# Fixed places for the splits and stores of weight forms, four rounded tiles in layer one, and token-form remainders on VectorE

## The chip, the cores and the metric

The kernel runs on one core of one Trainium2 chip. The metric is the device time of one execution in microseconds. The engines are called TensorE (PE), VectorE (DVE), ScalarE (ACT), GpSimd (POOL) and SyncE (SP); ScalarE and SyncE also issue the transfers of this kernel.

## What is computed

Attention in a window of 128 tokens with a linear bias (4 batches, 8 heads, 576 tokens, 64 per head), then a gated layer (512 to 1536 and back to 512) and a second layer whose two products are multiplied and go through two more weights:

```python
attn = softmax(where(mask, q @ k.T / 8 + bias, -1e9))     # 4 x 8 heads
x = (attn @ v).transpose(0, 2, 1, 3).reshape(2304, 512)
x = (sigmoid(x @ w_gate) * (x @ w_val)) @ w_out           # layer one, 1536 wide
out = ((x @ w1) * (x @ w2) @ w3) @ w_out2                 # layer two, 1024 wide
```

## The kernel before

**Precision.** A float32 operand is split into two parts that TensorE takes at full rate: `act_copy` (L79) writes the rounded high part on ScalarE, `dve_lo` (L82) or `pool_lo` (L85) subtracts it and writes the remainder on VectorE or GpSimd. Each product then has three passes (L31): high by high, high by low, low by high. Weights come as 64-bit words; `rounded` (L140) makes float32 of them with one ScalarE step (L146, absolute value) and six VectorE steps (L147 to L152) into a tile with the tag `ca`, of which there are two. Some weights are rounded ahead and stored to `early32` in DRAM; they come back as float32 (`raw32`).

**Stages.** Attention runs to about 180 us with parts of layer one beside it. Layer one (`gv`, `down1`) runs over slices 0 to 11 of its width, in groups of two, and five blocks of tokens of 256 or 512; the products `gv` go through a tanh (`g`, L364), a multiply (L371) and a split (`gt`), and `dn` adds into `acc` (L398). Near its end the fold (`fold`, L299) multiplies the two last weights into `outd`, and `x_forms(0)` makes sums and differences of the token blocks, split into `xf` (L422 to L426). With n = 0 its remainders go to GpSimd for B11, B21, T1 and T3, and to VectorE for the others.

**Layer two** runs over slices 12 to 19, twice (n = 0 with token blocks 1, 2 and 0, n = 1 with blocks 3 and 4). For each slice `products` (L454) forms seven products by a scheme that needs sums and differences of the weights: eight weight forms A21, A22, A11, A12, S1 to S4, kept as high and low parts in a tile `forms`. There are two such tiles, one for even and one for odd slices. The chunks of a slice follow one another on TensorE: `pb` with A11, `pd` with S1, `pb` with S2, `pb` with S3, `pc` with A12, `pb` with A22, `pd` with S4. Three of them add into the same bank, and ScalarE copies the bank in between: `x1` after A11, `xa` after S2, `xb` after S3. A chunk into `pb` can't start before the copy of what stood there. The products of x1 and of xa with xb are split into `tp` and `tq` (`turn`, L468) and feed the output products `o` (`down2`, L539), which stand between the chunks of the following slices. `lone` (L513) does block 0.

**How the forms come.** With n = 0 `form_sink` (L207) is called by `convert_next` (L155), right behind the rounding, for the slice two ahead of the one whose products were just issued. It splits A11 with A12 and A21 with A22, adds and subtracts on VectorE (L225 to L228) and splits S1 with S2 and S3 with S4: four ScalarE copies and four GpSimd subtracts. `keep` (L232) stores the forms to DRAM from ScalarE's queue, and `again` (L247) loads them for n = 1.

**What sets the order.** A planner puts the instructions of each engine in order by priority and by its own estimate of when they can start; each engine then works its queue in that order. `tc.high_priority(offset=SOONER)` moves instructions ahead, `LATER` (in `convert_next`) moves them back. `tc.issue_after(ins)` ties the instructions of a block that run on the engine of `ins` behind `ins` in that queue. Outside attention the order of TensorE too is the planner's.

Of the kernel before, what the change touches and what calls it, by code (L numbers as in the profile page):

```python
# [56 lines left out]
def attn_moe_kernel(  # L57
# [19 lines left out]
    NK = DM // P  # L77

    def act_copy(dst, src):  # L79
        nc.scalar.activation(dst, src, AF.Copy)  # L80

    def dve_lo(dst, src, hi):  # L82
        nc.vector.tensor_tensor(dst, src, hi.bitcast(F32), ALU.subtract)  # L83
# [1 line left out]
    def pool_lo(dst, src, hi):  # L85
        nc.gpsimd.tensor_tensor(dst, src, hi.bitcast(F32), ALU.subtract)  # L86
# [22 lines left out]
        return accpools[blk > 1].tile(shape, F32, tag=f"acc{blk}", name=f"{name}_{blk}")  # L109


    spool = None
    staged = {}
    rings = {"raw": 2, "raw32": 0, "ca": 2}
    held = {"raw": 0, "raw32": 0}
# [13 lines left out]
    def kind(src):  # L129
        return "raw32" if src.dtype == F32 else "raw"  # L130
# [9 lines left out]
    def rounded(t, key):  # L140

        low, high = t[:, :, 0], t[:, :, 1]
        a = spool.tile([P, DM], U32, name=f"a_{key}", tag="ca", bufs=rings["ca"])
        s = spool.tile([P, DM], U32, name=f"s_{key}", tag="cs", bufs=1)
        x, y = a.bitcast(F32), s.bitcast(F32)
        nc.scalar.activation(x, high.bitcast(F32), AF.Abs)  # L146
        nc.vector.tensor_scalar(x, x, bits(F64_LEAST), bits(F64_MOST), ALU.max, ALU.min)  # L147
        nc.vector.tensor_scalar(a, a, 0x07FFFFFF, 3, ALU.bitwise_and, ALU.logical_shift_left)
        nc.vector.scalar_tensor_tensor(a, high, 0xC0000000, a, ALU.bitwise_and, ALU.bitwise_or)
        nc.vector.tensor_scalar(s, a, 0xFF800000, None, ALU.bitwise_and)  # L150
        nc.vector.scalar_tensor_tensor(y, low, 2.0**-52, y, ALU.mult, ALU.mult)
        nc.vector.tensor_tensor(x, x, y, ALU.add)  # L152
        return x

    def convert_next():  # L155

        key, src, sink = queue.pop(0)
        with tc.high_priority(offset=-LATER):
            t = staged.pop(key)
            held[kind(src)] -= 1  # L160
            x = t if t.dtype == F32 else rounded(t, key)
            if sink is None:
                nc.sync.dma_start(ahead[key[1:]], x)
            elif (to := sink(key, x)) is not None:
                hi, lo = to
                act_copy(hi, x)
                (dve_lo if key[0] in ("o2", "w3") else pool_lo)(lo, x, hi)
        fetch_more()
# [17 lines left out]
    def parts(grp):  # L186
        def src(i, c):
            m = i - NF
            own = (w_gate, w_val, w_out)[c][i] if i < NF else (w1[m], w2[m])[c]
            return ahead.get((i, c), own)  # L190

        if grp[0] >= NF:
            return [((i, c), src(i, c), form_sink) for i in grp for c in range(2)]
        keys = [(i, c) for c in range(3) for i in grp]
        return [(key, src(*key), part_sink) for key in keys]

    forms = {}
    half = {}
    form_tiles = {}
    outw = {}  # L200

    def form_tile(i):
# [4 lines left out]
    def form_sink(key, x):  # L207

        i, c = key
        x = x.rearrange("p (b c) -> p b c", b=2)  # L210
        if c == 0:
            forms[i] = form_tile(i)
            half[i] = x
        w = forms[i]

        def split(at, src):
            hi, lo = w[:, at : at + 2, 0], w[:, at : at + 2, 1]
            act_copy(hi, src)
            pool_lo(lo, src, hi)

        split(A11 if c == 0 else A21, x)
        if c == 1:
            a = half.pop(i)
            s12, s34 = (upool.tile([P, 2, 2 * P], F32, name=f"s{k}_{i}", tag="cf", bufs=2) for k in (12, 34))
            nc.vector.tensor_tensor(s12[:, 0], x[:, 0], x[:, 1], ALU.add)  # L225
            nc.vector.tensor_tensor(s12[:, 1], s12[:, 0], a[:, 0], ALU.subtract)
            nc.vector.tensor_tensor(s34[:, 0], a[:, 0], x[:, 0], ALU.subtract)
            nc.vector.tensor_tensor(s34[:, 1], a[:, 1], s12[:, 1], ALU.subtract)  # L228
            split(S1, s12)
            split(S3, s34)  # L230
# [185 lines left out]
    def x_forms(n):  # L416

        p, q = (acc[blk] for blk in PAIRED[n])
        some_lo = dve_lo if n else pool_lo
        b11, b21, b12, b22 = p[:, 0:2], p[:, 2:4], q[:, 0:2], q[:, 2:4]  # L420

        def split(j, src, lo):  # L422
            t = xf[n, j] = xpool.tile([P, 2, 2, TB], F32R, name=f"xf{n}_{j}", tag=PLACES[n][j])
            for h in range(2):
                act_copy(t[:, 0, h], src[:, h])
                lo(t[:, 1, h], src[:, h], t[:, 0, h])  # L426

        def minus(to, x, y):
            for h in range(2):
                nc.vector.tensor_tensor(to[:, h], x[:, h], y[:, h], ALU.subtract)  # L430

        split(B11, b11, some_lo)
        yield
        split(B21, b21, some_lo)
        yield
        split(B22, b22, dve_lo)
        yield
        minus(b12, b12, b11)
        split(T1, b12, some_lo)
        yield  # L440
        minus(b22, b22, b12)
        split(T2, b22, dve_lo)
        yield
        minus(b11, b22, b11)
        split(T3, b11, some_lo)
        yield
        minus(b21, b21, b22)
        split(T4, b21, dve_lo)
        yield
# [4 lines left out]
    def products(n, i):  # L454

        def chunk(ps, a, j, first, last):
            for kk in range(2):
                for wp, xp in PASSES:
                    nc.tensor.matmul(  # L459
                        ps, forms[i][:, a, wp, kk * P : (kk + 1) * P], xf[n, j][:, xp, kk],  # L460
                        start=first and kk == 0 and (wp, xp) == PASSES[0],
                        stop=last and kk == 1 and (wp, xp) == PASSES[-1], skip_group_check=True,
                    )

        def bank(name, pool, tag):
            return pool.tile([P, TB], F32, tag=tag, name=f"{name}{n}_{i}", bufs=4)

        def turn(pr, name):  # L468
            t = m2.tile([P, 2, TB], F32R, tag="gt", name=f"{name}{n}_{i}", bufs=4)
            act_copy(t[:, 0], pr)  # L470
            pool_lo(t[:, 1], pr, t[:, 0])
            return t

        def now():
            return tc.high_priority(offset=SOONER)

        ts = ts2[n, i] = {}
        b, d = bank("pb", gvpool, gvtag), bank("pd", gvpool, gvtag)
        x1 = m2.tile([P, TB], F32, tag="g", name=f"x1_{n}_{i}")
        x2a, x2b = (upool.tile([P, TB], F32, tag="u", name=f"{nm}{n}_{i}") for nm in ("xa", "xb"))  # L480
        chunk(b, A11, B11, True, False)
        with now():
            act_copy(x1, b)
        yield 0
        chunk(d, S1, T1, True, False)
        yield 1
        chunk(b, S2, T2, False, False)
        with now():
            act_copy(x2a, b)
        yield 2  # L490
        chunk(b, S3, T3, False, False)
        with now():
            act_copy(x2b, b)
            nc.vector.tensor_tensor(x2b, x2b, d, ALU.add)
        yield 0
        c = bank("pc", mmpools[0], "mm")
        chunk(c, A12, B21, True, True)
        with now():
            nc.vector.tensor_tensor(x1, x1, c, ALU.add)
        yield 3  # L500
        chunk(b, A22, T4, False, True)
        with now():
            nc.vector.tensor_tensor(x1, x1, b, ALU.mult)
            ts[PAIRED[n][0]] = turn(x1, "tp")
        yield 1
        chunk(d, S4, B22, False, True)
        with now():
            nc.vector.tensor_tensor(x2a, x2a, d, ALU.add)
            nc.vector.tensor_tensor(x2a, x2a, x2b, ALU.mult)
            ts[PAIRED[n][1]] = turn(x2a, "tq")  # L510
        yield 1

    def lone(i):  # L513

# [321 lines left out]
        attention(actx, conv)  # L836


    rings.update({"raw": 3, "raw32": 4, "ca": 2})
    spool = ctx.enter_context(tc.tile_pool(name="conv1", bufs=1, reuse_waits="tile"))  # L840
    w3st = ExitStack()
    w3pool = w3st.enter_context(tc.tile_pool(name="w3pool", bufs=3, side="right", reuse_waits="tile"))
    w1st = ExitStack()
    wpools.append(w1st.enter_context(tc.tile_pool(name="wpool1", bufs=2, reuse_waits="tile")))
    gvpool = ctx.enter_context(tc.tile_pool(name="psgv", bufs=4, space=PSUM, reuse_waits="tile"))
    gvtag, gvbufs = "gv", 4
# [45 lines left out]
    flush()  # L892
    formpools = [None, None]
    w1st.close()
    upool = ctx.enter_context(tc.tile_pool(name="upool", bufs=3, reuse_waits="tile"))
    formpools[0] = ctx.enter_context(tc.tile_pool(name="forms0", bufs=1, reuse_waits="tile"))
    second = groups[last1 + 1 :]
# [16 lines left out]
    for n in range(len(PAIRED)):  # L914
        for g, grp in enumerate(second):
            final = n == 0 and g + 1 == len(second)
            for at, i in enumerate(grp):
# [3 lines left out]
                for gap in products(n, i):  # L921
# [3 lines left out]
                        step(alone)  # L925
                    if i == slices[-1] and n == 0:
                        step(xform)
                if n == 0:
                    with tc.issue_after(folded[NM - 1].ins):
                        keep(i)  # L930
                if at:
                    for _ in downs:
                        pass
# [64 lines left out]
```

## Time and profile before

| | us |
|---|---|
| median of 3 runs (lowest to highest) | 922.53 (921.52 to 926.82) |
| profiled execution | 922.87 |
| its span, first to last instruction | 921.2 |
| TensorE busy in the span | 877.7 |
| VectorE, ScalarE, GpSimd busy | 665.9, 352.4, 322.8 |

In the rows further down, a timeline has one line for each instruction (or for several alike): start in us, length in us, engine, line, operation, output `<-` inputs, shapes, count, and in brackets the idle time before it and what ended it. A mean clock of 1.00 is 2.4 GHz; 0.5 would be 1.2 GHz.

### The profile page before, as it was taken

The numbers are of one execution on the slowest core, as the hardware profiler recorded it, in microseconds if no ns is written. First come the engines' busy times: TensorE is split into PE (matmuls) and PEld (weight loads), VectorE is DVE, ScalarE is ACT, GpSimd is POOL, SyncE is SP. The second block draws the span as 40 slices with busy tenths as digits, with TensorE's granted clock in tenths as the row PEclk, the third lists the DMA queues.
The fourth block names the chain that finished last, engine by engine and source line by source line (L and its number), as shares of the span: only waits on it lengthen the run. The fifth ranks groups of instructions, "written<-read, shape, count | busy, mean of one in ns | idle before, by whom it ended". The sixth has DMA issues, their size and how long they took to land. (4 is left out here: it accounts for less than half of the span.)

```text
span 921.2 us, 12491 instructions
## 1 busy us (share of the span) xinstructions
PE 877.7 (95%) x4432; PEld 718.6 (78%) x4432; DVE 665.9 (72%) x1148; ACT 352.4 (38%) x853; POOL 322.8 (35%) x360
## 2 busy tenths in 40 slices
PE   6788998999999999999999899999989999999998
PEld 4556776788888888888888788878877788888886
DVE  6879898579994985986898872794587748534444
ACT  6878666533322322322332343443433324122120
POOL 4766554543312312412321223224744332112121
PEclk7899898999999999999999999999999999999999
DMA  5445352243440341251245441238454143655322
GB/s 200 144 144 183 116 187 80 77 141 106 139 159 1 115 153 42 86 164 60 69 129 168 148 138 38 78 128 316 185 206 148 82 168 95 227 192 175 105 102 92
DMA packets 40623, 121.67 MB, mean 132 GB/s; under 512 B 4464, under 2 KB 6512, under 8 KB 38512
## 3 DMA queue, kind: packets, MB, share of 16 engines
q1 hardware_dynamic: 39264, 106.05, 35.0%
q10 hardware_dynamic: 1296, 14.81, 3.8%
q8 instruction: 35, 0.57, 0.3%
q14 instruction: 28, 0.23, 0.1%
HBM read 88.34 MB, written 32.51 MB: 131 GB/s over the span
## 5 line engine op out<-in xcount | busy, mean ns | idle before, releaser
L347 PE MATMUL gv<-xth,wsl 128*128 128x512 f32 (+1 forms) x960 | 283.1, 373 | 3.3 <-DVE g L371 2.5
L347 PEld LDWEIGHTS gv<-xth,wsl 128*128 128x128 f32 x960 | 177.4, 192 | 37.4 <-issue 3.0
L347 PE MATMUL gv<-xtl,wsl 128*128 128x512 f32 (+1 forms) x480 | 178.4, 372 | 0.4 <-DVE xtl L83 0.4
L388 PE MATMUL dn<-gt,wsl 128*128 128x512 f32 (+1 forms) x720 | 157.4, 372 | 10.8 <-DVE xtl L83 4.5
L86 POOL TENSOR_TENSOR gt<-g,gt 128x512 fp32r<-128x512 f32 (+1 forms) x60 | 76.3, 1274 | 244.2 <-ACT gt L80 244.1
L388 PEld LDWEIGHTS dn<-gt,wsl 128*128 128x128 f32 x720 | 126.4, 190 | 36.7 <-issue 5.7
L459 PE MATMUL pb<-xf,forms 128*128 128x512 f32 x384 | 99.6, 396 | 6.7 <-ACT xa L80 5.3
L347 PEld LDWEIGHTS gv<-xtl,wsl 128*128 128x128 f32 x480 | 92.2, 192 | 15.9 <-DVE xtl L83 1.2
L459 PEld LDWEIGHTS pb<-xf,forms 128*128 128x128 f32 x384 | 71.2, 190 | 23.1 <-ACT xa L80 7.2
L398 DVE TENSOR_TENSOR acc<-acc,dn 128x512 f32<-128x512 f32 (+1 forms) x120 | 73.4, 626 | 19.5 <-PE dn L388 19.5
L80 ACT ACTIVATE gt<-g 128x512 fp32r<-128x512 f32 (+1 forms) x60 | 35.2, 588 | 96.2 <-DVE g L371 96.2
L559 DVE TENSOR_TENSOR acc<-acc,o 128x512 f32<-128x512 f32 x54 | 36.7, 684 | 39.7 <-PE o L549 39.4
L712 ACT ACTIVATE sm<-sm,mn 128x128 f32<-128x128 f32 x144 | 55.8, 390 | 19.0 <-DVE mn L709 12.9
L371 DVE SCALAR_TENSOR_TENSOR g<-g,gv 128x512 f32<-128x512 f32 (+1 forms) x60 | 37.5, 628 | 35.1 <-PE gv L347 32.4
L86 POOL TENSOR_TENSOR tp<-x,tp 128x512 fp32r<-128x512 f32 x16 | 21.8, 1361 | 94.9 <-ACT tp L80 94.9
L459 PE MATMUL pd<-xf,forms 128*128 128x512 f32 x192 | 48.7, 389 | 0.0
L549 PE MATMUL o<-outw,tp 128*128 128x512 f32 x192 | 47.7, 390 | 0.3 <-POOL tp L86 0.3
L549 PE MATMUL o<-outw,tq 128*128 128x512 f32 x192 | 47.9, 389 | 0.0
L364 ACT ACTIVATE g<-gv 128x512 f32<-128x512 f32 (+1 forms) x60 | 31.9, 546 | 40.9 <-PE gv L347 36.6
L720 POOL TENSOR_SCALAR sm<-sm,su 128x128 f32<-128x128 f32 x72 | 31.8, 453 | 42.7 <-DVE su L716 37.3
L308 PE MATMUL w3o<-wo,w3s 128*128 128x512 f32 x192 | 44.0, 389 | 0.0
L549 PEld LDWEIGHTS o<-outw,tp 128*128 128x128 f32 x192 | 36.0, 188 | 8.2 <-POOL tp L86 0.7
(798 smaller groups left out, 1468.9 us busy)
## 6 DMA issues: line engine op xcount, KB each, us to landing
formd<-forms ACTq DMA_DIRECT2D x8, 1792.0 KB, 6.4
outw<-outd SPq DMA_DIRECT2D x16, 512.0 KB, 6.0
forms<-formd SPq DMA_DIRECT2D x8, 1024.0 KB, 5.2
ldk<-in_k_dram SPq DMA_DIRECT2D x16, 320.0 KB, 3.7
ldv<-in_v_dram SPq DMA_DIRECT2D x16, 320.0 KB, 3.0
out_dram<-acc SPq DMA_DIRECT2D x18, 256.0 KB, 2.0
ldq<-in_q_dram SPq DMA_DIRECT2D x16, 256.0 KB, 4.0
outd<-w3o SPq DMA_DIRECT2D x8, 512.0 KB, 3.4
```

The costliest lines, as they stand in the source:

```text
L80: nc.scalar.activation(dst, src, AF.Copy)
L86: nc.gpsimd.tensor_tensor(dst, src, hi.bitcast(F32), ALU.subtract)
L308: nc.tensor.matmul(acc2, w3s[u][:, wp, i * P : (i + 1) * P], wo2[kk][:, xp], start=(kk == 0 and wp == 0 and xp == 0), stop=(kk == NC2 - 1 ...
L347: nc.tensor.matmul(ps, wsl[i][:, s, wp, kk * P : (kk + 1) * P], xs[blk][xp][:, kk], start=(kk == 0 and wp == 0 and xp == 0), stop=(kk == N ...
L364: nc.scalar.activation(g[i], pss[i, 0], AF.Tanh, scale=0.5)
L371: nc.vector.scalar_tensor_tensor(pr, pr, 1.0, pss[i, 1], ALU.add, ALU.mult)
L388: nc.tensor.matmul(ps, wsl[i][:, 2, wp, m * P : (m + 1) * P], t[:, xp], start=n == 0, stop=n == 3 * len(grp) - 1,)
L398: nc.vector.tensor_tensor(a, a, ps, ALU.add)
L459: nc.tensor.matmul(ps, forms[i][:, a, wp, kk * P : (kk + 1) * P], xf[n, j][:, xp, kk], start=first and kk == 0 and (wp, xp) == PASSES[0], ...
L549: nc.tensor.matmul(ps, ts2[n, i][blk][:, xp, tt * P : (tt + 1) * P], outw[i][:, wp], start=k == 0, stop=k == 3 * len(grp) - 1,)
L559: nc.vector.tensor_tensor(a, a, ps, ALU.add)
L712: s["act"] = nc.scalar.activation(y, y, AF.Exp, bias=mn[:, j : j + 1], scale=1.0 / up, accum_out=su[:, j : j + 1])
```

## The change

For slices 14 to 19, `form_sink` now only keeps the two tiles, and the splits are issued by `make_forms` during the products of the slice before: behind the copy `xb` of slices 14 to 18, and for slice 14 behind the copy `x1` of slice 13. `keep` of slices 14 to 19 is tied behind the copy `xa` of the same slice (that of 12 and 13 behind the last fold, as before). A raw tile that a waiting split still reads counts as held until then. The split of the second product into `tq` is issued behind the next slice's copy `x1`, in both passes, but for the last slice. In layer one there are four tiles `ca` in a pool of their own, and two in layer two. The remainders of all `xf` of `x_forms(0)` are on VectorE.

```diff
     def rounded(t, key):
-        a = spool.tile([P, DM], U32, name=f"a_{key}", tag="ca", bufs=rings["ca"])
+        a = (capool or spool).tile([P, DM], U32, name=f"a_{key}", tag="ca", bufs=rings["ca"])
     def convert_next():
-            held[kind(src)] -= 1
+            if not (kind(src) == "raw32" and sink is form_sink and key[0] > NF + 1):
+                held[kind(src)] -= 1
     def form_sink(key, x):
+        if i > NF + 1:
+            if c == 1:
+                waiting[i] = lambda: (form_part(i, 0, half[i]), form_part(i, 1, x))
+        else:
+            form_part(i, c, x)
+
+    def form_part(i, c, x):
         w = forms[i]
...
     def x_forms(n):
-        some_lo = dve_lo if n else pool_lo
+        some_lo = dve_lo
...
         chunk(b, A11, B11, True, False)
         with now():
-            act_copy(x1, b)
+            copied = act_copy(x1, b)
+        if n == 0 and i == NF + 1:
+            make_forms(i + 1, copied)
+        while late:
+            with now(), tc.issue_after(copied.ins):
+                late.pop(0)()
...
         chunk(b, S2, T2, False, False)
         with now():
-            act_copy(x2a, b)
+            copied = act_copy(x2a, b)
+        if n == 0:
+            with tc.issue_after((copied if i > NF + 1 else folded[NM - 1]).ins):
+                keep(i)
         yield 2
         chunk(b, S3, T3, False, False)
         with now():
-            act_copy(x2b, b)
+            copied = act_copy(x2b, b)
             nc.vector.tensor_tensor(x2b, x2b, d, ALU.add)
+        if n == 0 and NF + 1 < i < NF + NM - 1:
+            make_forms(i + 1, copied)
...
             nc.vector.tensor_tensor(x2a, x2a, x2b, ALU.mult)
-            ts[PAIRED[n][1]] = turn(x2a, "tq")
+            ts[PAIRED[n][1]] = t = m2.tile([P, 2, TB], F32R, tag="gt", name=f"tq{n}_{i}", bufs=4)
+
+        def turn_later():
+            act_copy(t[:, 0], x2a)
+            pool_lo(t[:, 1], x2a, t[:, 0])
+
+        if i == NF + NM - 1:
+            with now():
+                turn_later()
+        else:
+            late.append(turn_later)
...
+    def make_forms(i, after):
+        with tc.issue_after(after.ins):
+            waiting.pop(i)()
+        for c in range(2):
+            if parts_of[i, c] == "raw32":
+                held["raw32"] -= 1
+        fetch_more()
...
-    rings.update({"raw": 3, "raw32": 4, "ca": 2})
+    rings.update({"raw": 3, "raw32": 4, "ca": 4})
     spool = ctx.enter_context(tc.tile_pool(name="conv1", bufs=1, reuse_waits="tile"))
+    w1st = ExitStack()
+    capool = w1st.enter_context(tc.tile_pool(name="capool1", bufs=1, reuse_waits="tile"))
...
     w1st.close()
+    rings["ca"] = 2
+    capool = ctx.enter_context(tc.tile_pool(name="capool2", bufs=1, reuse_waits="tile"))
...
-                if n == 0:
-                    with tc.issue_after(folded[NM - 1].ins):
-                        keep(i)
```

## Rows read from the trace of the kernel before

**Rows 1.** The page's head: span, then busy us, share and instructions of each engine.

```profile
span 921.2 us, 12491 instructions
...
PE 877.7 (95%) x4432; PEld 718.6 (78%) x4432; DVE 665.9 (72%) x1148; ACT 352.4 (38%) x853; POOL 322.8 (35%) x360
```

**Rows 2.** Table of stretches: from:to us, length, busy us of engines, granted clock, transfers.

```profile
250.00:510.00 260.00, 260.00 (x1250) 219.65 (x1249) 210.72 (x345) 74.72 (x127) 70.07 (x53) 1.00 0.34 107
...
520.00:530.00 10.00, 7.47 (x49) 7.18 (x48) 8.56 (x16) 3.46 (x7) 3.01 (x2) 0.84 0.43 145
...
690.00:700.00 10.00, 9.65 (x41) 8.06 (x42) 5.26 (x10) 3.49 (x7) 4.10 (x4) 0.83 0.00 0
```

**Rows 3.** Waits of TensorE, 250 us to the end: us in total, times, longest.

```profile
PE pb L459 <- ACT xa L80: 5.3, 3, 2.4
PE gv L347 <- DVE g L371: 2.5, 1, 2.5
PE pb L459 <- ACT xb L80: 1.4, 1, 1.4
PE dn L388 <- DVE acc L398: 1.4, 1, 1.4
```

**Rows 4.** Timeline of all engines in slices 15 and 16, 680 to 712 us.

```profile
683.20 1.78 DVE L152 TENSOR_TENSOR a_(17, 0)_6430<-a_(17, 0)_6430,s_(17, 0)_6431 128x512 f32<-128x512 f32 x1
...
688.68 0.41 DVE L226 TENSOR_TENSOR s<-s,a_(17, 0)_6430 128x256 f32<-128x256 f32 x1
...
689.18 0.63 ACT L80 ACTIVATE forms<-s 128x512 fp32r<-128x512 f32 x1 [5.94 <-issue]
689.71 0.58 ACT L80 ACTIVATE xa<-pb 128x512 f32<-128x512 f32 x1
...
690.35 2.67 PE L459 MATMUL pb<-xf,forms 128*128 128x512 f32 x6 [2.37 <-ACT xa L80]
...
695.95 0.68 ACT L146 ACTIVATE a_(18, 0)_6603<-raw_(18, 0)_6293 128x512 f32<-128x512 f32 x1 [1.41 <-POOL forms L86]
```

**Rows 5.** Timeline of TensorE, 700 us to the end: A11 of slices 16, 17.

```profile
702.40 1.52 PE L459 MATMUL pb<-xf,forms 128*128 128x512 f32 x6
...
723.30 1.52 PE L459 MATMUL pb<-xf,forms 128*128 128x512 f32 x6
```

**Rows 6.** Timeline of ScalarE, 555 to 665 us: slices 12 and 13.

```profile
644.46 0.63 ACT L80 ACTIVATE forms<-raw_(14, 0)_5875 128x512 fp32r<-128x512 f32 x1 [1.45 <-DMA formd<-forms]
...
645.51 0.58 ACT L80 ACTIVATE xb<-pb 128x512 f32<-128x512 f32 x1
```

**Rows 7.** Timeline of all engines in layer one, 505 to 545 us.

```profile
522.51 0.67 ACT L146 ACTIVATE a_('w3', 7)_5548<-raw_('w3', 7)_5242 128x512 f32<-128x512 f32 x1 [3.56 <-DMA early<-_('ahead', 'w3', 5)_5079]
...
525.21 0.68 DVE L371 SCALAR_TENSOR_TENSOR g<-g,gv 128x512 f32<-128x512 f32 x1
```

**Rows 8.** Timeline of VectorE, 555 to 665 us: end of layer one.

```profile
590.07 1.25 DVE L430 TENSOR_TENSOR acc<-acc,acc 128x512 f32<-128x512 f32 x1
...
605.68 0.68 DVE L83 TENSOR_TENSOR w3s<-raw_('w3', 10)_5521,w3s 128x512 fp32r<-128x512 f32 x1
606.28 0.68 DVE L398 TENSOR_TENSOR acc<-acc,dn 128x512 f32<-128x512 f32 x1
```

**Rows 9.** Timelines of VectorE, ScalarE and GpSimd in slice 16, 706 to 747 us.

```profile
709.20 0.69 DVE L152 TENSOR_TENSOR a_(18, 1)_6616<-a_(18, 1)_6616,s_(18, 1)_6617 128x512 f32<-128x512 f32 x1
...
714.56 0.60 ACT L80 ACTIVATE xb<-pb 128x512 f32<-128x512 f32 x1 [1.47 <-PE pb L459]
...
715.75 1.29 POOL L86 TENSOR_TENSOR forms<-a_(18, 0)_6603,forms 128x512 fp32r<-128x512 f32 x1 [2.02 <-ACT forms L80]
```

**Rows 10.** Groups of VectorE, 588 to 612 us: count, busy us, mean ns.

```profile
L430 DVE TENSOR_TENSOR acc<-acc,acc 128x512 f32<-128x512 f32 x6 | 6.8, 1144 | 0.1
...
L83 DVE TENSOR_TENSOR xf<-acc,xf 128x512 fp32r<-128x512 f32 x6 | 4.9, 831 | 0.0
L430 DVE TENSOR_TENSOR acc<-acc 128x512 f32<-128x512 f32 x2 | 1.4, 688 | 0.0
```

More of the change, by code (lines that the diff above doesn't have):

```diff
@@ L79, in act_copy @@
     def act_copy(dst, src):
-        nc.scalar.activation(dst, src, AF.Copy)
+        return nc.scalar.activation(dst, src, AF.Copy)
     def dve_lo(dst, src, hi):
@@ L109, in acc_tile @@
         return accpools[blk > 1].tile(shape, F32, tag=f"acc{blk}", name=f"{name}_{blk}")
-    spool = None
+    spool = capool = None
     staged = {}
@@ L192, in parts @@
         if grp[0] >= NF:
+            parts_of.update({(i, c): kind(src(i, c)) for i in grp for c in range(2)})
             return [((i, c), src(i, c), form_sink) for i in grp for c in range(2)]
@@ L197, in attn_moe_kernel @@
     forms = {}
+    parts_of = {}
     half = {}
     form_tiles = {}
+    waiting = {}
+    late = []
     outw = {}
@@ L836, in attn_moe_kernel @@
         attention(actx, conv)
-    rings.update({"raw": 3, "raw32": 4, "ca": 2})
+    rings.update({"raw": 3, "raw32": 4, "ca": 4})
     spool = ctx.enter_context(tc.tile_pool(name="conv1", bufs=1, reuse_waits="tile"))
+    w1st = ExitStack()
+    capool = w1st.enter_context(tc.tile_pool(name="capool1", bufs=1, reuse_waits="tile"))
     w3st = ExitStack()
     w3pool = w3st.enter_context(tc.tile_pool(name="w3pool", bufs=3, side="right", reuse_waits="tile"))
-    w1st = ExitStack()
     wpools.append(w1st.enter_context(tc.tile_pool(name="wpool1", bufs=2, reuse_waits="tile")))
```

## The prediction

> **What bounds the kernel now.** I read the page's head first: TensorE is busy 877.7 of 921.2 us [rows 1]. Next came the table of stretches, because an average share hides where the idle time lies. From 250 to 510 us TensorE is busy all the time at a granted clock of 1.00 [rows 2]. So a change to the other engines can gain only in between, and only by ending a wait of TensorE. The list of TensorE's waits from 250 us to the end has four entries over half a microsecond: 5.3 us (three waits) on the copy `xa`, 2.5 on `g`, 1.4 on `xb` and 1.4 on `acc` [rows 3], 10.6 us in sum. The first 180 us, the attention, come before anything that the diff touches.
>
> Idle time is not the whole price. In 520 to 530 us the granted clock is 0.84, in 690 to 700 us it is 0.83 [rows 2]; TensorE had just idled 2.5 and 2.4 us. Part of each stretch thus ran at 1.2 GHz instead of 2.4. That loses 10 x 0.16 = 1.6 and 10 x 0.17 = 1.7 us. The matmuls agree: the six `pb` after the second wait take 2.67 us [rows 4], six of the same kind without a wait 1.52 [rows 5], so 1.15 of the 1.7 us are seen there. What the change can reach is 10.6 + 1.6 + 1.7 = 13.9 us.
>
> Who is late, wait by wait? In slice 15 (679 to 702 us) ScalarE idles 5.94 us and then runs, first, a split `forms<-s` at 689.18 and, behind it, the copy `xa<-pb` at 689.71 [rows 4]. The split belongs to slice 17. It waited for VectorE, whose `s` (L226) ran from 688.68 to 689.09 because rounding stood ahead of it, one step of which (L152) took 1.78 us beside a GpSimd subtract [rows 4]. The copy itself was only queued behind that split, and TensorE's next six `pb` (S3) need the copy. Slices 16 and 17 repeat this, with 5.3 - 2.4 = 2.9 us between them. At 644.46 a split of slice 14 waits 1.45 us for the store of slice 12's forms, and the copy `xb` runs only at 645.51 [rows 6]: the 1.4 us. At 522.51 the rounding's first step waits 3.56 us on ScalarE for a store to `early`, which still holds one of two rounded tiles; VectorE's rounding and behind it the multiply `g` (525.21) follow, and TensorE waits 2.5 us for it [rows 3, 7]. At 606.28 the addition to `acc` that frees a PSUM bank stands behind splits on VectorE [rows 8], which held the last `dn` by 1.4 us.
>
> **The change, part by part.** *Splits behind fixed copies (slices 14 to 19).* No split of slices 14 to 19 is issued two slices ahead any more. Those of slice i+1 follow slice i's copy `xb` (for slice 14, slice 13's copy `x1`). No instruction is added or removed. In slices 15, 16 and 17 nothing that waits for VectorE's rounding is then in front of `xa`. Gain: 5.3 + 1.7 = 7.0 us. The cost must be sought in slice i+1: a slice lasts 723.30 - 702.40 = 20.9 us [rows 5]; the copy `xb` ends about 12.8 us into it (714.56 + 0.60 - 702.40) [rows 5, 9]. Then come four ScalarE copies of 0.63 us [rows 4] and four GpSimd subtracts of some 1.3 us [rows 9], with the subtracts of `tp` and `t` between them: 4 x 1.3 + 1.3 + 0.7 (half the width, so an estimate of half the time) = 7.2 us. That ends 20 us into the slice, in time for slice i+1, which needs only A11 first, S1 1.4 us later and the rest 6 us or more later. So I cost it at nothing; the cover is the tail of slice i.
>
> The rounding must then be done when the splits come. For slice 18 it ran from 695.95 to 709.20 + 0.69, or 13.9 us [rows 4, 9]. Its two tiles come free some 3 us after one `xb` and are wanted at the next, so there are 20.9 - 3 = 17.9 us. Slack: 4 us.
>
> *Stores.* `keep(i)` of slices 14 to 19 now stands behind `xa` of the same slice on ScalarE's queue. By then its forms have long been written, so it waits for nothing; it goes past `xb`, by the length of one issue. The store reads tiles that are overwritten a slice and a half later. SP's queue keeps its order. Cost: nothing; cover: the products between S3 and A22. Slices 12 and 13 keep their old tie to the fold. The store of slice 12 therefore lands as late as before (644.4 us), and the splits of slice 14 still need it. Only what stands behind them may differ. The gain on that 1.4 us lies between 0 and 1.4. I take 0, since the row that ends that wait is not touched.
>
> *The copy `tq` behind the next slice's `x1`.* `x1` of the next slice stood behind `tq`, which waits for VectorE's product. Now it comes first, so S2 can follow S1 sooner. `tq` is wanted only by the later half of the output products. Gain on the path: none shown beyond the 7.0; cost: 0.
>
> *Four rounded tiles in layer one.* The wait of 3.56 us for a slot goes, as two more are free. VectorE's four rounding steps in front of `g` start that much earlier, more than TensorE's 2.53 us of idling. Gain: 2.5 + 1.6 = 4.1 us. From below: 0, if another instruction becomes late in its place, and even a loss of as much, since more rounding may now be in VectorE's queue ahead of a `g`.
>
> *Remainders on VectorE.* Eight subtracts `xf` go from GpSimd (1.3 us each by its other subtracts) to VectorE (0.68) [rows 8, 9]. Four of them stood at 563 to 569 us, where VectorE is nearly idle. The other four fall in 588 to 612 us, where VectorE has no pause. Adding: VectorE's splits there start 0.60 us apart (605.68, 606.28) [rows 8], so 4 x 0.60 = 2.4 us. Removing: beside GpSimd's subtracts the six L430 take 1144 ns on average against 688 undisturbed, the six `xf` 831 against 680 [rows 8, 10]: 6 x 0.456 + 6 x 0.151 = 3.6 us. Some 0.5 of it is the L430 at 590.07 (1.25 us instead of 0.69) [rows 8], which lies beside a `gt` subtract that stays. Net 3.1 - 2.4 = 0.7 us earlier. The wait of 1.4 us falls to 0.7. Bounds: all of it goes (+1.4), or no relief comes and it grows by 2.4.
>
> The Trainium skill (page "SBUF — State Buffer", section "Who interferes with whom") says that a VectorE instruction with two SBUF inputs and a GpSimd instruction that reads SBUF block one another whole, whichever starts first. The 1.78 us beside a GpSimd subtract agree with it [rows 4]. By the rule alone the slices' splits, now in one run on GpSimd, would delay VectorE's rounding more than before, which is the rival below on late rounding.
>
> **The sum.** 7.0 + 0 + 4.1 + 0.7 = 11.8 us. The profiled execution took 922.87 us, its span 921.2; 922.87 - 11.8 = 911.1. The median of the three runs is 0.34 lower, so 910.7.
>
> **The rivals.** (1) *Layer one keeps a wait.* The order of every queue is made anew by the planner, and VectorE is busy 210.7 of 260 us there [rows 2]. Another `g` may come late. Against it: fewer things wait for stores. Time: 910.7 + 4.1 = 914.8. (2) *The change does only part of its work in layer two*: each of slices 14 to 18 keeps a short wait of another kind, say at A22 for `xb`, of 1.4 us, like the two waits of slices 16 and 17 (2.9 / 2). Five of them cost 7.0: 917.7. (3) *Nothing is gained*: both happen, 921.8. (4) *Slower: late rounding blocks ScalarE at the fixed place.* The splits of slice i+1 now stand in front of `tp`, `t` and the next `x1`. If the rounding ends late by more than its 4 us and the 8 us from `xb` to the next slice, slices 16 to 19 each start late. Slice 17's rounding needed 13.9 us; from 26 us on it decides. Each start that is late by 3 us costs 3 + 1.7, four of them 18.8; without the 7.0 of this part, that is 910.7 + 7.0 + 18.8 = 936.5. For it: one such split idled ScalarE 5.94 us. Against it: VectorE has pauses in these slices, so 26 us is far.
>
> The Trainium skill (page "TensorE: Matmul & The Clock Gate", section "Architectural detail: the array is 16× 32×32, not 1× 128×128") says that ScalarE's queue is strictly first in, first out. It speaks for rival 4, as a fixed place cannot be passed when its data are late; the 5.94 us with `xa` behind them agree [rows 4].
>
> **How the numbers follow.** Forecast 0.55; rival 1 0.18; rival 2 0.09; rival 3 0.10; rival 4 0.08. The forecast's own bounds: 1.4 less at slice 12's store and 0.7 less at `acc` give 908.6, and 1.7 to 2.4 more at `acc` 913.1; below, the ceiling of 13.9 gives 908.6 too. The range runs from 908 to 918, which takes in rivals 1 and 2 and leaves 0.18 out. Half a percent (4.6 us) is about what a measurement of this kernel can tell from no change; the bounds are 917.9 and 927.1. Faster: 0.55 + 0.18 + 0.09 = 0.82, less 0.02 because rival 2 lies at the bound: 0.80. Same 0.12, slower 0.08.
>
> **What would show it.** In the profile after, TensorE's list of waits should have lost `xa` and `g`, keep at most 1.4 us on `xb`, and `acc` below 1.4. No stretch behind 250 us should have a granted clock under 0.95. On ScalarE, `xa<-pb` should directly follow its product in slices 15 to 17, the splits should stand behind `xb`, and `xf` should have no GpSimd row. It is wrong if new waits of TensorE for `forms`, `g` or `o` banks sum to over 7 us, or if ScalarE idles at a split longer than the 8 us of cover.

## The result

The changed kernel takes 910.71 us (median of 4 runs, 908.61 to 911.74), the kernel before 923.36 beside it (4 runs). The ratio is 0.9856, 95% interval 0.982 to 0.9892. The profiled execution took 909.88 us, its span is 908.2. The forecast was 910.7.

The head of the page after, which answers to [rows 1]:

```profile
span 908.2 us, 12508 instructions
...
PE 872.8 (96%) x4432; PEld 715.5 (79%) x4432; DVE 661.1 (73%) x1156; ACT 351.8 (39%) x853; POOL 313.3 (35%) x352
```

The waits of TensorE from 180 us to the end (us in total, times, longest), which answer to [rows 3]:

```profile
PE pd L472 <- DVE xb L515: 0.8, 1, 0.8
PE w3o L321 <- ACT w3s L80: 0.4, 1, 0.4
PE o L591 <- POOL tp L86: 0.3, 1, 0.3
```

None of the four waits of before is left. Two small ones are new (0.8 and 0.4 us); the one on `tp` stood there before as well. The stretches of [rows 2] now read:

```profile
250.00:510.00 260.00, 260.00 (x1250) 219.63 (x1249) 213.70 (x361) 75.73 (x131) 73.10 (x52) 1.00 0.34 114
...
520.00:530.00 10.00, 10.00 (x68) 9.25 (x67) 8.52 (x14) 6.25 (x14) 3.56 (x4) 1.00 0.50 153
...
690.00:700.00 10.00, 10.00 (x46) 8.28 (x45) 9.86 (x16) 2.52 (x5) 3.73 (x4) 1.00 0.35 112
```

TensorE is busy through both 10 us stretches at a granted clock of 1.00, where it was 0.84 and 0.83; no other stretch of 10 us behind 250 us is below 1.00 either. ScalarE in slices 15 and 16 (A11 of slice 16 ends a little before 694.82), which answers to [rows 4, 9]:

```profile
683.84 0.60 ACT L80 ACTIVATE xb<-pb 128x512 f32<-128x512 f32 x1 [0.94 <-PE pb L472]
684.33 0.62 ACT L80 ACTIVATE forms<-a_(16, 0)_6264 128x512 fp32r<-128x512 f32 x1
...
698.90 0.60 ACT L80 ACTIVATE xa<-pb 128x512 f32<-128x512 f32 x1 [2.18 <-PE pb L472]
...
703.08 0.60 ACT L80 ACTIVATE xb<-pb 128x512 f32<-128x512 f32 x1 [0.94 <-PE pb L472]
703.57 0.62 ACT L80 ACTIVATE forms<-a_(17, 0)_6435 128x512 fp32r<-128x512 f32 x1
704.09 0.62 ACT L80 ACTIVATE forms<-a_(17, 1)_6446 128x512 fp32r<-128x512 f32 x1
704.62 1.14 ACT L80 ACTIVATE forms<-s 128x512 fp32r<-128x512 f32 x2
```

`xa` (698.90) follows its product with no split in front of it, and the four splits of slice 17 stand directly behind `xb`.

To see where the 13.0 us of span come from, I cut every profile of this study at the same three places: the start of a `dn` product near 244 us, the start of slice 12's copy `x1`, and the end of the span. "Layer one" is the second minus the first, "layer two" the third minus the second, all from the timelines of TensorE and ScalarE. Each profile is of one execution, which can lie up to 3.3 us off the median (e3's took 914.97 us, its median is 911.66). Ratios compare the median with that of runs of the kernel before taken beside them.

| kernel | `dn` | `x1` of 12 | span | layer one | layer two | ratio (95%) |
|---|---|---|---|---|---|---|
| before | 244.09 | 634.55 | 921.2 | 390.5 | 286.7 | |
| after | 244.70 | 630.00 | 908.2 | 385.3 | 278.2 | 0.9856 (0.982 to 0.9892) |
| e1, splits loose | 245.13 | 630.90 | 910.2 | 385.8 | 279.3 | 0.9885 (0.9855 to 0.9915) |
| e2, two tiles | 243.83 | 635.49 | 913.7 | 391.7 | 278.2 | 0.9918 (0.9889 to 0.9946) |
| e3, `xf` on GpSimd | 245.94 | 632.24 | 913.3 | 386.3 | 281.1 | 0.9889 (0.9851 to 0.9928) |
| e4, `tq` at once | 245.64 | 631.20 | 909.8 | 385.6 | 278.6 | 0.987 (0.9833 to 0.9907) |
| e5, e1 and e4 | 243.10 | 629.81 | 913.7 | 386.7 | 283.9 | 0.9924 (0.99 to 0.9948) |
| e6, before + fixed places | 244.31 | 636.15 | 914.7 | 391.8 | 278.6 | 0.9928 (0.9905 to 0.9951) |
| e7, before + later `tq` | 243.86 | 636.28 | 925.5 | 392.4 | 289.2 | 1.0032 (1.0011 to 1.0052) |
| e8, before + four tiles | 243.82 | 631.60 | 922.0 | 387.8 | 290.4 | 1.0022 (0.9997 to 1.0046) |
| e9, before + store's place | 245.79 | 635.63 | 917.2 | 389.8 | 281.6 | 0.9947 (0.9929 to 0.9965) |
| e10, store at the end | 242.98 | 629.58 | 907.6 | 386.6 | 278.0 | 0.9864 (0.9833 to 0.9896) |
| e11, more rounding | 243.88 | 629.34 | 917.4 | 385.5 | 288.1 | 0.9962 (0.9943 to 0.9981) |
| e12, before + `xf` on VectorE | 245.57 | 633.94 | 918.9 | 388.4 | 285.0 | 0.998 (0.9964 to 0.9996) |

From before to after, layer one gives 5.2 us and layer two 8.5; the start is 0.6 later, and the start differs by up to 3 us between kernels that are alike there.

### The profile page after: what moved, and what is told of

It reads as the page before. It is cut to its first block, busy times and chain, and to the rows that moved or that the text cites. A ratio compares the mean times of both kernels' runs of the same rounds, so it can differ in the third digit from the quotient of the medians.

```text
span 908.2 us, 12508 instructions
## 1 busy us (share of the span) xinstructions
PE 872.8 (96%) x4432; PEld 715.5 (79%) x4432; DVE 661.1 (73%) x1156; ACT 351.8 (39%) x853; POOL 313.3 (35%) x352
## 4 chain that ended last, share of the span: by engine, by line
PE 80%; DVE 12%; ACT 3%; POOL 2%; issue 2%; DMA 0%; SPq 0%; ACTq 0%; DVEq 0%; POOLq 0%
PE gv L360 30%; PE dn L401 14%; PE o L591 11%; PE pb L472 9%; PE pd L472 4%; PE w3o L321 3%; PE lone L565 3%; PE pc L472 2%; PE pv L795 2%; DVE s L738 2%; ACT sm L754 2%; DVE sm L741 2%; DVE mn L747 1%; PE pt L772 1%; PE s L730 1%
## 5 line engine op out<-in xcount | busy, mean ns | idle before, releaser
L86 POOL TENSOR_TENSOR gt<-g,gt 128x512 fp32r<-128x512 f32 (+1 forms) x60 | 79.3, 1324 | 250.8 <-ACT gt L80 250.8
L401 PE MATMUL dn<-gt,wsl 128*128 128x512 f32 (+1 forms) x720 | 155.0, 369 | 8.4 <-DVE xtl L83 5.2
L472 PE MATMUL pb<-xf,forms 128*128 128x512 f32 x384 | 97.7, 391 | 0.0
L754 ACT ACTIVATE sm<-sm,mn 128x128 f32<-128x128 f32 x144 | 55.8, 390 | 18.1 <-DVE mn L751 12.7
L795 PE MATMUL pv<-cp,ldv 128*64 128x256 f32 (+1 forms) x352 | 40.8, 373 | 3.2 <-POOL cp L780 3.2
```

The source lines that it names most:

```text
L401: nc.tensor.matmul(ps, wsl[i][:, 2, wp, m * P : (m + 1) * P], t[:, xp], start=n == 0, stop=n == 3 * len(grp) - 1,)
L472: nc.tensor.matmul(ps, forms[i][:, a, wp, kk * P : (kk + 1) * P], xf[n, j][:, xp, kk], start=first and kk == 0 and (wp, xp) == PASSES[0], ...
L754: s["act"] = nc.scalar.activation(y, y, AF.Exp, bias=mn[:, j : j + 1], scale=1.0 / up, accum_out=su[:, j : j + 1])
L795: nc.tensor.matmul(ps[c, a:b], loads[n]["v"][:, j + 1, c], s["cp", h][:, m0 : m0 + b - a], start=j == -back, stop=j == nt - 1, skip_group_ ...
```

## The experiments

Theory A is the prediction's: loose splits in front of the copies, a slot of the rounding ring, and GpSimd's subtracts made the waits. Its rivals were that the later `tq` (B) or the order coming out of layer one (C) took them away, and later that the store's place alone does (D).

**e1: the splits are loose again.** In the changed kernel:

```diff
-        if i > NF + 1:
-            if c == 1:
-                waiting[i] = lambda: (form_part(i, 0, half[i]), form_part(i, 1, x))
-        else:
-            form_part(i, c, x)
+        form_part(i, c, x)
...
-            make_forms(i + 1, copied)
```

Both calls of `make_forms` go, and a raw tile no longer counts as held for a waiting split.

> The changed kernel, but the splits of slices 14 to 19 are issued right behind the rounding again, two slices ahead and tied to nothing; all else of the change stays. If the splits in front of the copies cost the time (theory A), waits of TensorE on the copies `xa` and `xb` come back: three of 5.3 us in sum with 1.7 us of lower clock, so 7 us more than the changed kernel, about 917.5. If the later place of `tq` brought the gain in layer two (theory B), because S2 then follows S1 sooner and S3 has more room, the time stays within 2 us of the changed kernel, about 911.

Measured: 911.51 us, none of the waits on `xa`; the longest is on VectorE's `xb`:

```profile
PE pd L467 <- DVE xb L508: 1.9, 1, 1.9
```

The fixed splits can be undone with hardly any loss. That spoke against theory A as it stood: something else in the change keeps `xa` free as well.

**e2: two rounded tiles in layer one.**

```diff
-    rings.update({"raw": 3, "raw32": 4, "ca": 4})
+    rings.update({"raw": 3, "raw32": 4, "ca": 2})
```

> The changed kernel, but with two rounded tiles in layer one instead of four. Theory A: the wait of TensorE on `g` near 523 us comes back, 2.5 us and 1.6 us by the lower clock behind it, so about 914.8. Rival: the order of the queues made that wait, and the order is new anyway; then no such wait shows and the time is that of the changed kernel, about 911.

Measured: 913.73 us. The longest wait of TensorE from 180 us on:

```profile
PE gv L360 <- DVE g L384: 3.9, 1, 3.9
```

The wait is back, with 3.9 us instead of 2.5, and only layer one is longer (391.7 against 385.3). Beside the wait, the granted clock is 0.77 in 520 to 530 us and 0.89 in the next 10 us. Inside the whole change the four tiles are worth 6.4 us of this profile's layer one; by the medians of e2 and e4, 913.73 - 910.56 = 3.2 us. The rival falls.

**e3: remainders on GpSimd.**

```diff
-        some_lo = dve_lo
+        some_lo = dve_lo if n else pool_lo
```

> The changed kernel, but the remainders of B11, B21, T1 and T3 are on GpSimd again. Theory A (the subtracts on GpSimd hold up VectorE's two-input subtracts): the wait of TensorE on `acc` near 605 us comes back with 1.4 us, so 0.7 to 1.4 us more than the changed kernel, 911.5 to 912.5, which the time alone can't tell and the list of waits can. Rival (the order of VectorE's queue, not its load, made that wait): no wait on `acc`.

Measured: 911.66 us. The longest waits of TensorE:

```profile
PE pb L472 <- ACT xb L80: 1.1, 1, 1.1
PE pd L472 <- DVE xa L531: 0.9, 1, 0.9
PE dn L401 <- DVE acc L411: 0.7, 1, 0.7
```

The wait on `acc` comes back, with half of the 1.4 us expected. More comes from layer two (281.1 against 278.2): 2.0 us of waits around slice 13, and a granted clock of 0.94 between 640 and 660 us. Neither account had that.

**e4: `tq` at once.**

```diff
-        if i == NF + NM - 1:
-            with now():
-                turn_later()
-        else:
-            late.append(turn_later)
+        with now():
+            turn_later()
```

> The changed kernel, but every slice's `tq` is split at once, ahead of the next slice's copy `x1`. Theory A: the copy `x1` comes some 2 us later, which is covered by TensorE's other products; no wait, time within 1 us of the changed kernel, about 911. Theory B (the later `tq` brought part of the gain): waits of TensorE for copies come back, 2 to 7 us more, 913 to 918.

Measured: 910.56 us, and the list of waits is that of the changed kernel. Beside the fixed splits the later `tq` brings nothing.

**e5: both undone,** e1's and e4's edits together.

> The changed kernel with both undone at once: the splits of the forms tied to nothing, two slices ahead, and every `tq` split at once. Theory A2 (either of the two is enough to keep TensorE from waiting for `xa`): with both gone the three waits return, 5.3 us and 1.7 us of lower clock, about 7 us over the changed kernel, 917 to 918. Theory C (the order that comes out of layer one, by four tiles and the remainders on VectorE, moved the rounding of slices 16 to 19 away from the copies): no such waits, 911 to 912.

Measured: 914.56 us, 3 to 4 us over e1 (by the medians and by the ratios). There are waits of 2.1 us on `x` and 1.9 us on `xb`, but still none on `xa`, so neither theory's number fits. ScalarE's timeline shows why, in slice 15:

```profile
682.71 0.60 ACT L80 ACTIVATE xa<-pb 128x512 f32<-128x512 f32 x1 [1.75 <-PE pb L467]
682.71 0.33 ACTq L242 DMA_DIRECT2D formd<-forms  x1
...
686.89 0.60 ACT L80 ACTIVATE xb<-pb 128x512 f32<-128x512 f32 x1 [1.00 <-PE pb L467]
690.06 0.63 ACT L80 ACTIVATE forms<-a_(17, 0)_6437 128x512 fp32r<-128x512 f32 x1 [2.58 <-DMA formd<-forms]
```

The split (690.06) waits for a store of forms to land, which was issued at 682.71, behind `xa`. In before the stores were issued one slice earlier, right behind the splits. This kernel still has the store's new place, and a split can't overwrite forms that the store hasn't read. So the store holds the splits back, past `xa` and `xb`. That is theory D; e9 tests it alone.

**e6: before with fixed splits and stores only.** The changed kernel with e4's and e3's edits and a single ring of two tiles.

> The kernel before with one part alone: splits and stores of the forms behind the fixed copies; two tiles, `tq` at once, remainders on GpSimd as before. Theory A2: the three waits on `xa` go (7.0 us), the wait on `g` (4.1 with its clock) and on `acc` stay, so 922.5 - 7.0 = 915.5, 914 if the wait on `xb` goes too. Theory C: waits on `xa` remain, 921 to 923.

Measured: 915.65 us. The longest waits of TensorE:

```profile
PE gv L360 <- DVE g L384: 3.9, 1, 3.9
PE dn L401 <- DVE acc L411: 1.4, 1, 1.4
PE pd L472 <- DVE xb L515: 0.8, 1, 0.8
```

All three waits on `xa` are gone and those of layer one stay, as theory A said; layer two takes 278.6 us, within 0.4 of the changed kernel. Theory C falls: no new order out of layer one is needed. This edit holds the store's new place too, so it doesn't price the fixed splits alone.

**e7: before with the later `tq` only.** The edits of e1 and e3, two tiles, and the store back in its old place:

```diff
-        if n == 0:
-            with tc.issue_after((copied if i > NF + 1 else folded[NM - 1]).ins):
-                keep(i)
...
+                if n == 0:
+                    with tc.issue_after(folded[NM - 1].ins):
+                        keep(i)
```

> The kernel before with one part alone: `tq` split behind the next slice's copy `x1`; forms as before. Theory A2: the three waits on `xa` go here too, about 915.5, because TensorE's S2 follows S1 sooner and S3 then has other products in front of it. Theory A of the first runs or theory C: the waits stay, 921 to 923.

Measured: 925.54 us, slower than before by 0.1 to 0.5%. The longest waits of TensorE:

```profile
PE pb L467 <- ACT xa L80: 6.4, 3, 2.7
PE gv L355 <- DVE g L379: 3.3, 1, 3.3
PE pb L467 <- ACT xb L80: 1.6, 1, 1.6
```

The waits on `xa` grow from 5.3 to 6.4 us. Theory B, and that either part is enough, fall.

**e8: before with four tiles only.** The edits of e1, e3 and e4, and e7's store.

> The kernel before with one part alone: four rounded tiles in layer one, two in layer two. Theory A2: the wait on `g` goes (2.5 us and 1.6 us by the clock), the waits on `xa` stay, 922.5 - 4.1 = 918.4. Theory C: the waits on `xa` go as well, about 911 to 912.

Measured: 924.64 us, no gain (the interval holds 1). The longest waits of TensorE:

```profile
PE pb L467 <- ACT xa L80: 7.7, 4, 2.4
PE pb L467 <- ACT xb L80: 2.6, 1, 2.6
PE gv L355 <- DVE g L379: 1.5, 2, 1.0
```

The wait on `g` shrinks, layer one is 2.7 us shorter, and layer two 3.7 longer: `xa` is waited for four times instead of three, `xb` 2.6 us instead of 1.4. The gain is given back in layer two as long as the splits are loose. Why the new order hurts just there was not settled. For `xb` the trace shows how: the split of slice 14 waits 2.60 us for the store of slice 12's forms (1.45 in before), with `xb` behind it.

**e9: before with the store's place only.** The edits of e1, e3 and e4, and two tiles; the store stays behind `xa`.

> The kernel before with one step alone: the store of slice i's forms (14 to 19) tied behind the copy `xa` of slice i, where it stood behind the splits one slice earlier; the splits stay loose. Theory D: the later store holds back the splits that overwrite those forms until it lands, past `xa` and `xb`, so the three waits on `xa` go as with the fixed splits: 3 to 7 us less than before, 915 to 919. Rival (the waits went in e1 and e5 by the order that comes out of layer one): waits on `xa` stay, 921 to 924.

Measured: 917.97 us, ratio 0.9947. The list of waits has no `xa`; its longest:

```profile
PE pb L467 <- ACT x L80: 2.1, 3, 1.0
PE gv L355 <- DVE g L379: 2.0, 1, 2.0
PE pb L467 <- ACT xb L80: 1.6, 1, 1.6
```

ScalarE in slice 15 shows the split of slice 17 held by the store, behind `xb`:

```profile
690.47 0.60 ACT L80 ACTIVATE xb<-pb 128x512 f32<-128x512 f32 x1 [1.00 <-PE pb L467]
693.62 0.63 ACT L80 ACTIVATE forms<-a_(17, 0)_6430 128x512 fp32r<-128x512 f32 x1 [2.55 <-DMA formd<-forms]
```

Theory D holds: tying the store behind `xa` is enough to keep loose splits off `xa`, for 5.1 us of layer two; waits on `x` take back a part.

**e10: the changed kernel with the store in its old place** (e7's diff alone).

> The changed kernel, but the stores are tied to the last fold only, as before. Theory D: the fixed splits alone keep `xa` free; no wait on `xa`, time within 1 us of the changed kernel, about 911. Rival: the stores' place is what does it; waits of some 5 us return, 916 to 918.

Measured: 910.23 us, ratio 0.9864 against 0.9856, layer two 278.0. The longest waits of TensorE:

```profile
PE o L588 <- POOL tp L86: 0.9, 2, 0.6
PE gv L360 <- DVE g L384: 0.8, 2, 0.5
```

ScalarE starts the splits of slice 17 at 703.01, behind `xb` at 702.51, so none of them stands in front of `xa`. Either step by itself keeps `xa` free; the fixed splits don't need the store's new place. One control is missing: no run has loose splits and the old place of the stores with all other parts of the change. That this one would wait for `xa` is inferred from e7, e8 and e12, which have one of those parts each and keep three or four such waits.

**e11: more rounding.** In `rounded`, for slices 16 to 19:

```diff
+        if not isinstance(key[0], str) and key[0] >= NF + 4:
+            for _ in range(4):
+                nc.vector.tensor_scalar(s, a, 0xFF800000, None, ALU.bitwise_and)
```

> The changed kernel with one step of the rounding (L150's, which gives the same value again) done four times more for each tile of slices 16 to 19: 8 x 0.43 = 3.4 us more VectorE work in each of slices 15 to 18. The rounding of slice 17 ends 1.8 us ahead of its splits in the changed kernel, so it would end 1.6 us late. Prediction's term: the tail of the slice covers that, no wait of TensorE, time within 1 us of the changed kernel, about 911. Rival 4: ScalarE idles at the fixed place with `tp`, `t` and the next `x1` behind it, slices start late: 2 us or more for each of three slices, 917 or more.

Measured: 919.53 us. The cover doesn't hold. ScalarE at the fixed place of slice 16:

```profile
705.89 0.60 ACT L80 ACTIVATE xb<-pb 128x512 f32<-128x512 f32 x1 [0.94 <-PE pb L475]
706.39 0.62 ACT L80 ACTIVATE forms<-a_(17, 0)_6443 128x512 fp32r<-128x512 f32 x1
709.80 0.63 ACT L80 ACTIVATE forms<-a_(17, 1)_6458 128x512 fp32r<-128x512 f32 x1 [2.78 <-DVE a_(17, 1)_6458 L155]
712.15 0.63 ACT L80 ACTIVATE forms<-s 128x512 fp32r<-128x512 f32 x1 [1.73 <-DVE s L242]
```

It idles 2.78 us for the rounding, as rival 4 said. But TensorE doesn't wait for ScalarE's copies in these slices. VectorE in the same stretch, then TensorE:

```profile
707.38 1.66 DVE L154 SCALAR_TENSOR_TENSOR s_(17, 1)_6459<-raw_(17, 1)_6277,s_(17, 1)_6459 128x512 f32<-128x512 uint32 x1
...
710.60 1.52 DVE L242 TENSOR_TENSOR s<-s,a_(17, 0)_6443 128x256 f32<-128x256 f32 x1
712.04 0.68 DVE L525 TENSOR_TENSOR x<-x,pc 128x512 f32<-128x512 f32 x1
```

```profile
712.77 1.66 PE L594 MATMUL o<-outw,tp 128*128 128x512 f32 x6 [1.38 <-DVE x L525]
...
734.60 1.65 PE L594 MATMUL o<-outw,t 128*128 128x512 f32 x6 [2.12 <-DVE x L525]
...
755.39 1.66 PE L594 MATMUL o<-outw,tp 128*128 128x512 f32 x6 [1.09 <-DVE x L525]
```

The addition `x<-x,pc` (712.04) frees the bank that TensorE's `o` needs, and it stands behind the lengthened rounding and the sums for the splits, some of them stretched beside GpSimd's subtracts. Three waits of 4.6 us in sum. Another 3.0 us are waits near 653 to 655 and 757 us; those near 653 to 655 come before the late splits, in an order that the longer rounding changed, and the granted clock there is 0.83 (650 to 660 us). So of some 9 us, 4.6 are shown to be the late rounding's own, through VectorE's queue rather than ScalarE's.

**e12: before with remainders on VectorE only.** The edits of e1 and e4, two tiles, and e7's store.

> The kernel before with one part alone: the remainders of B11, B21, T1 and T3 on VectorE. By the prediction's term the wait on `acc` falls from 1.4 to 0.7 us or less and all else stays: 0.7 to 1.4 us less than before, about 921. If the order of layer two hangs on it (rival), the waits on `xa` change too, by 2 us or more either way.

Measured: 920.77 us, ratio 0.998. The wait on `acc` is gone, the waits on `xa` stay:

```profile
PE pb L467 <- ACT xa L80: 5.5, 3, 2.4
```

Layer one is 388.4 us, 2.1 less than before. The prediction's term is borne out in its sign and place; its size was 0.7, and all of the 1.4 us went.

## Why the prediction was right, point by point

That the median of 910.71 us lies 0.01 us from the forecast is luck. The gain was 12.65 us against a sum of 11.8, and the kernel before took 923.36 us beside it against the 922.53 that I had started from: two misses of about 0.8 us that cancel.

**What bounds the kernel** held. The 13.0 us are waits of TensorE and what its clock lost behind them. Waits fell from 10.6 to 1.2 us, not counting `tp`: 9.4; the two stretches at a lower clock give 3.3. That is 12.7, and the start 0.6 later takes it to 12.1. The other 0.9 us lie in TensorE's busy time in layer two, which fell by 2.6 us (275.93 to 273.35) where the clock accounts for 1.7; what they are stays open.

**Fixed splits, 7.0 us.** The mechanism is shown: e6 has no wait on `xa`, with 8.1 us of layer two, and e10 has none without the store's new place. The cover held: GpSimd ends the splits of slice 17 at 709.40, ahead of that slice's A11 at 712.50. The size was low by the next point.

**The wait on `xb` in slice 12, taken as 0 of 1.4.** This term was wrong. The split of slice 14 no longer stands in front of that copy, so the store of slice 12 doesn't matter to it. I had also taken the landing of that store as fixed, and it isn't: in e1 and e5 the loose split of slice 14 runs 8.4 us behind slice 12's `x1` without waiting for it, where before it had waited until 9.9 us behind. A wait of 0.8 us on VectorE's `xb` one slice later takes back part. Net 0.6.

**Stores, costed at nothing.** Right for the sum, wrong as a reading: I asked whether the store waits, not who waits for the store. Its later place holds back loose splits and is worth 4.8 us by itself (e9, 922.79 - 917.97). Beside the fixed splits it adds nothing (e10), so the sum didn't show the miss.

**The later `tq`, 0.** Right beside the fixed splits (e4). Alone it costs 3.7 us (e7, 1.0 to 4.8 by its interval), and with loose splits held back by the store it saves 3 to 4 (e5 against e1): the waits of 2.1 us on `x` in e5 and e9, where `x` stands behind `tq`, are not in e1. It isn't a part with a price of its own.

**Four tiles, 4.1 us, bounds from a loss of as much.** The wait on `g` went (in e8, with four tiles alone, 1.5 us of shorter ones remain). Its size isn't fixed, though: with two tiles it measured 2.5, 3.9, 3.9, 3.3, 2.0 and 2.2 us (before, e2, e6, e7, e9, e12), since a store's landing ends it: in these six ScalarE's rounding step in front waits 3.0 to 4.4 us for a store to `early`. The term of 4.1 lies between what e8 (2.7) and e2 (6.4) show for layer one; the medians of e2 and e4 give 3.2.

**Remainders on VectorE, 0.7 of 1.4.** All of it went (e12 and after); after has a new wait of 0.4 us on `w3s`, which e12 has not. My upper bound for this term was mis-added: 2.4 us more instead of 0.7 less is 3.1, so 913.8 us and not 913.1. I also overlooked that the tiles act on this wait: with the remainders on GpSimd it is 1.3 to 1.4 us with two tiles (e6, e7, e9) and 0.7 with four (e3, e8). VectorE at that place, where [rows 8] had the addition at 606.28:

```profile
598.32 1.28 DVE L443 TENSOR_TENSOR acc<-acc,acc 128x512 f32<-128x512 f32 x2
...
600.12 0.68 DVE L411 TENSOR_TENSOR acc<-acc,dn 128x512 f32<-128x512 f32 x1
```

Two L430 (L443 now) take 1.28 us in sum, so GpSimd no longer stretches them; the mean of all six is 685 ns, where it was 1144 [rows 10]. This is what the rule of the Trainium skill (page "SBUF — State Buffer", section "Who interferes with whom") leads one to expect.

**The cover of the rounding.** The slack was 1.8 us, not 4. (The 13.9 us that rival 4 gives for slice 17 are slice 18's.) Slice 17's rounding in the changed kernel:

```profile
688.84 0.65 ACT L146 ACTIVATE a_(17, 0)_6435<-raw_(17, 0)_5909 128x512 f32<-128x512 f32 x1
```

```profile
701.12 0.68 DVE L152 TENSOR_TENSOR a_(17, 1)_6446<-a_(17, 1)_6446,s_(17, 1)_6447 128x512 f32<-128x512 f32 x1
```

It runs from 688.84 to 701.80 and the splits start at 703.57. I had let it begin 3 us behind `xb`; it begins 5 us behind (683.84 to 688.84), since the planner puts it behind `t`. The further 8 us of cover I had counted aren't there (e11): I followed ScalarE's queue and left out that VectorE's other work stands behind the rounding too.

The sum was 11.8 us against 13.0 of the profile and 12.65 of the medians. Two terms were low by 0.6 and 0.7, less the new wait of 0.4; the others held in sum.

## What to carry to other kernels

A stall of the busiest engine is worth what its list of waits says plus what the clock lost behind it, but parts of a change that guard the same queue don't add. Alone, the fixed places of splits and stores gave 6.2 us, where the store's place by itself already gave 4.8; the remainders gave 2.0, the four tiles nothing clear of noise, and the later `tq` cost 3.7. Together they gave 12.65. When an instruction is moved, ask not only what it waits for but who waits for it; here a later store did the work of a fixed place. And a fixed place is only as good as the engine that feeds it: measure its slack, then look at what stands behind the late work on that engine's own queue.

## What was not expected of the hardware

The clock's price of one wait isn't fixed. In before a wait of 2.37 us at slice 15 was followed by a stretch at 0.83 of the full clock. The same wait, of about 2.4 us, left the clock at 1.00 in e8 and e12:

```profile
690.00:700.00 10.00, 7.63 (x40) 6.37 (x39) 6.15 (x13) 4.13 (x8) 3.29 (x4) 1.00 0.12 45
```

```profile
680.00:700.00 20.00, 17.64 (x90) 14.70 (x89) 16.07 (x25) 7.00 (x13) 8.46 (x7) 1.00 0.35 136
```

Other waits show it too. The one on `g` took 3.9 us in e2 and in e6, and in 520 to 530 us the granted clock was 0.77 in one and 0.89 in the other. The one on VectorE's `xb` took 1.9 us in e1 and in e5, and in 640 to 650 us the clock was 1.00 in one and 0.83 in the other. So the 1.7 us that I added belong to this execution, not to the wait; from these traces the term lies between 0 and 1.7. What decides it was not tested.
